# First block's states decayed on their way out of PSUM, and a work list drawn up 30 more times

## The chip, the cores and the metric

The kernel runs as one launch on 1 core of a Trainium2 chip. The metric is device time in microseconds, the median of several runs; lower is better. The engines of the core run side by side and wait for one another by semaphores: TensorE (PE in the profile, its weight loads PEld), VectorE (DVE), ScalarE (ACT), GpSimd (POOL), and SyncE (SP), which here issues every DMA.

## The reference

Three stages follow one another on 3072 tokens (4 batches of 768) with 512 features. First comes a retention attention with 8 heads of 64:

```python
state = np.zeros((B, H, D, D), dtype=np.float32)
for t in range(S):
    state = gamma[None, :, None, None] * state + np.einsum('bhd,bhe->bhde', k[:, :, t], v[:, :, t])
    y[:, :, t] = scale * np.einsum('bhd,bhde->bhe', q[:, :, t], state)
```

Then comes a layer 512 -> 2048 -> 512, whose hidden value h becomes h above 1, 0 below -1 and (h+1)^2/4 between. Then comes a layer 512 -> 1024 -> 512 with h * softmax(h), normalised to mean 0 and variance 1 and scaled by g_ln, ahead of the second product.

## The kernel before

The tokens are cut into 6 chunks of 128 per batch; chunk c of all 4 batches makes up block c. A unit u is one chunk of one batch: units 0 to 3 are block 0, 4 to 7 block 1, 8 to 15 blocks 2 and 3 (two batches of a pair are worked half a chunk at a time), and units 16 to 23 are done two at a time as "wide" steps in blocks 4 and 5. Within a unit, attention is a product of scores and values (with a table of decays, `dmat`), plus, from block 1 on, a "cross" product of the queries with the state that earlier chunks left.

The running state of each batch lies in `states`. Decay is spread over several tables: `vdec` scales keys, `xdec` is the loaded table of decays of the queries or outputs, `qdec` is `xdec` times the decay over 128 tokens (`gdec`), `gdec2` is that decay laid out for a state, and `gdec4` its square. In the kernel before:

- block 0 ends with one copy on ACT of a unit's state from PSUM (L819);
- block 1 multiplies its queries by `qdec` (L650 and L652), because the state has not been decayed yet; when block 1 adds its own sum to the state, the old state is first scaled by `gdec2` in 4 pieces on ACT (L804), and then the sum is added on DVE (L805);
- blocks 3 and 5 first multiply the state by `gdec4` on DVE (L541, in `counted_on`), so the states are held two chunks at a time; even blocks take values scaled by `vgrow` and outputs scaled by `qdec`, odd ones values scaled by `vdec` and outputs scaled by `xdec`;
- `qdec` is loaded as a copy of the table and multiplied by `gdec` on POOL (L480), early; `xdec` is loaded a second time, later (L493).

While block 0 to 3 of attention run, the first layer's products for blocks 0 and 1 (L1068 into, L1142 out) and the conversion of the weights to two parts (L393 to L428) run as well. Blocks 2 to 5 then go through a seven-product scheme (L1324, L1477), and the last layer follows (L1819, L1930, L1962).

The order on each engine is fixed when the program is built. Every piece of work is a `Task` with an engine, a cost, the tasks it depends on and a buffer that it takes. `Plan.late` walks back from the planned products of PE and gives each other task a goal, the time by which it is wanted. `Plan.listed` then plays the engines forward by the costs and always takes the ready task with the earliest goal; products of PE may be taken a few places early in the first and last parts (`loose`). `Plan.run` does this 4 times, each time with goals worked out from the list before, and keeps the list whose reckoned end of PE is earliest. The instructions are then written out in that order, and each engine works strictly in order. POOL and those DVE tasks that depend on no PE product are kept apart in the list (`port`).

Of the kernel before, what the change touches and what calls it, by code (L numbers as in the profile page):

```python
# [24 lines left out]
C = 128  # L25
# [69 lines left out]
class Plan:  # L95
# [32 lines left out]
    def run(self, rounds=4):  # L128
        best, edges, order = None, {}, list(self.tasks)
        for _ in range(rounds):  # L130
            self.late(order, edges)
            try:
                end, order, edges = self.listed()
            except RuntimeError:
                if best is None:
                    raise
                break
            if best is None or end < best[0]:
                best = end, order, [(t, t.start, t.end) for t in order]
# [126 lines left out]
def kernel(  # L266
# [189 lines left out]
    def tables():  # L456
# [21 lines left out]
        b = DMA(2, lambda: nc.sync.dma_start(gdec, gdec_d), (), -50.0)  # L478
        q = DMA(256, lambda: nc.sync.dma_start(qdec, xtab_d), (), -50.0)
        tab["qdec1"] = [POOL(1.05, lambda: gp.tensor_tensor(out=qdec, in0=qdec, in1=gdec.to_broadcast([128, NPAIR, C]), op=ALU.mult), (b, q), -48.0)]  # L480
# [5 lines left out]
    def late_tables():  # L486
# [6 lines left out]
        tab["xdec"] = [DMA(256, lambda: nc.sync.dma_start(xdec, xtab_d))]  # L493
# [9 lines left out]
    def out_factors(c):  # L503
        return (xdec, tab["xdec"]) if c % 2 else (qdec, tab["qdec1"])
# [5 lines left out]
    def scaled_values(c, p, o, swapped):  # L510
        t, deps = ((vdec2, "vdec2") if swapped else (vdec, "vdec")) if c % 2 else ((vgrow2, "vgrow2") if swapped else (vgrow, "vgrow"))
# [25 lines left out]
    def counted_on(c, pair):  # L537

        st = states[pair]
        if c % 2:  # L540
            st_wrote[pair] = [DVE(U512, lambda: ve.tensor_tensor(out=st, in0=st, in1=gdec4.to_broadcast([128, 2, NPAIR, D]), op=ALU.mult), [*st_wrote[pair], *tab["gdec4"]])]  # L541
# [87 lines left out]
    def att_scores0(u):  # L629
# [12 lines left out]
        if u >= CPB:  # L642
# [3 lines left out]
            def f():  # L646
                e["qn"] = attp.tile([128, NPAIR, C], F32, tag="qn", name="qn", bufs=NQN)
                q = e["qk"][:, 0]
                if not o:
                    ve.tensor_tensor(out=e["qn"], in0=q, in1=qdec, op=ALU.mult)  # L650
                for r in range(2) if o else ():
                    ve.tensor_tensor(out=e["qn"][64 - 64 * r:128 - 64 * r], in0=q[64 * r:64 * r + 64], in1=qdec[64 * r:64 * r + 64], op=ALU.mult)  # L652
            e["qn_task"] = DVE((1 + o) * U512, f, [e["lq"]] + tab["qdec1"], t.vend + 1, (e["qn_slot"],))
# [72 lines left out]
    def att_steps0(u):  # L726
# [76 lines left out]
        if blk:  # L803
            dec = [ACT(A64, partial(lambda p: sc.activation(st[:, p], st[:, p], AF.Copy, scale=gdec2[:, b % 2, p, :]), p), [ta] + tab["gdec"]) for p in range(NPAIR)]  # L804
            x = DVE(U256, lambda: ve.tensor_tensor(out=st, in0=e["sp"], in1=st, op=ALU.add), [tb, *dec])  # L805
# [1264 lines left out]
```

## Time and profile before

| what | us |
|---|---|
| median of 3 runs (lowest, highest) | 844.01 (843.34, 844.15) |
| the profiled execution's own time | 842.65 |
| its span, first to last instruction | 840.7 |
| PE busy | 827.5 (98%) |
| DVE busy | 679.8 (81%) |
| ACT busy | 566.6 (67%) |
| POOL busy | 133.4 (16%) |

The profiled execution took 1.95 us more than its span, and 1.36 us less than the median of the runs. A busy share says how long an engine had work under way; the end of the program is set by PE's order of products and by the gaps between them.

### The profile page before, as it was taken

Reading aid. Unit: us, or ns where it says so; the run is one execution under the profiler, and the core shown is the slowest. Engines: PE = TensorE matmul, PEld = TensorE weight load, DVE = VectorE, ACT = ScalarE, POOL = GpSimd, SP = SyncE. Lnnn points to the kernel's source line nnn. Section 1 sums busy time; section 2 is a strip of 40 time slices with the busy share of each in tenths; the row PEclk is TensorE's granted clock in tenths of the full one; section 3 lists DMA queues with packets and bytes.
Section 4 is the critical chain, followed back from the end, with each engine's and each line's share of the span. In section 5 each row is a group of like instructions: output and inputs, shape, how many; then the busy total and the mean of one; then the engine's idle time right before and its main releaser. Section 6 shows DMA issues by size and latency. Waiting matters only on the chain.

```text
span 840.7 us, 15941 instructions
## 1 busy us (share of the span) xinstructions
PE 827.5 (98%) x5872; PEld 677.1 (81%) x5872; DVE 679.8 (81%) x1299; ACT 566.6 (67%) x1107; POOL 133.4 (16%) x403
## 2 busy tenths in 40 slices
PE   9999999999999999999999999999999999999997
PEld 7778888777878888888888788887888888888885
DVE  6999999999857678999996397898777777777751
ACT  3898977897799898874588685445555555555552
POOL 1100000000000000001200000022473333333443
PEclk9999999999999999999999999999999999999999
DMA  8967999998999999876765555764202012021011
GB/s 329 399 214 242 320 313 322 335 323 301 335 374 335 347 345 327 327 282 238 228 216 196 200 197 188 265 196 159 69 33 75 27 40 61 18 71 24 15 39 37
DMA packets 66145, 175.72 MB, mean 209 GB/s; under 512 B 8338, under 2 KB 12562, under 8 KB 66068
## 3 DMA queue, kind: packets, MB, share of 16 engines
q1 hardware_dynamic: 66068, 174.71, 60.0%
q8 instruction: 46, 0.75, 0.4%
q14 instruction: 31, 0.25, 0.1%
HBM read 124.35 MB, written 50.33 MB: 208 GB/s over the span
## 4 chain that ended last, share of the span: by engine, by line
PE 67%; DVE 18%; ACT 7%; DMA 5%; issue 2%; SPq 0%; ACTq 0%; DVEq 0%
PE hp L1324 17%; PE op L1962 16%; PE yp L1477 14%; PE h2p L1819 13%; PE tp L1930 2%; PE acc L1142 2%; DMA w_raw<-in_w_in_dram 2%; DVE wm L409 2%; DVE wm L406 1%; DMA x2p<-cs 1%; DVE w L428 1%; DVE go L1444 1%; PE hp L1068 1%; DVE cs L1050 1%; DVE gl L1099 1%
## 5 line engine op out<-in xcount | busy, mean ns | idle before, releaser
L1477 PE MATMUL yp<-go,left 128*128 128x512 f32 x672 | 153.0, 389 | 0.0
L1477 PEld LDWEIGHTS yp<-go,left 128*128 128x128 f32 x672 | 126.1, 188 | 26.2
L1324 PE MATMUL hp<-xoh,left 128*128 128x512 f32 x448 | 121.8, 394 | 0.6 <-DVE g L1050 0.4
L1440 ACT ACTIVATE go<-g 128x512 fp32r<-128x512 f32 x112 | 69.8, 629 | 51.4 <-PE yp L1477 30.3
L1324 PEld LDWEIGHTS hp<-xoh,left 128*128 128x128 f32 x448 | 82.9, 188 | 19.3 <-ACT hp L1352 1.1
L1962 PE MATMUL op<-w,lh 128*128 128x512 f32 x384 | 93.5, 391 | 0.8 <-ACT lh L1937 0.8
L1819 PE MATMUL h2p<-w,x2h 128*128 128x512 f32 x336 | 92.3, 396 | 0.5 <-ACT h2p L1832 0.4
L1509 POOL TENSOR_TENSOR gl<-gl,gh 128x512 f32<-128x512 f32 x4 | 6.5, 1636 | 504.4 <-DVE gl L1506 373.4
L1962 PEld LDWEIGHTS op<-w,lh 128*128 128x128 f32 x384 | 71.9, 188 | 16.5 <-ACT lh L1937 1.5
L1444 DVE TENSOR_TENSOR go<-g,go 128x512 fp32r<-128x512 f32 x112 | 76.9, 691 | 8.2 <-ACT go L1440 7.5
L1142 PE MATMUL acc<-gh,w 128*128 128x512 f32 x256 | 69.9, 402 | 2.0 <-ACT gh L1095 1.2
L1819 PEld LDWEIGHTS h2p<-w,x2h 128*128 128x128 f32 x336 | 61.3, 188 | 13.0 <-ACT h2p L1832 1.1
L1324 PE MATMUL hp<-xol,left 128*128 128x512 f32 x224 | 69.0, 389 | 0.0
L1068 PE MATMUL hp<-xh,w 128*128 128x512 f32 x248 | 62.6, 393 | 0.6 <-DVE w L428 0.6
L1881 DVE TENSOR_REDUCE st<-h2p 128x1 f32<-128x512 f32 x24 | 16.5, 686 | 57.1 <-PE h2p L1819 57.1
L1049 ACT ACTIVATE cs<-cs 128x512 f32<-128x512 f32 x96 | 59.2, 625 | 0.9
L1142 PEld LDWEIGHTS acc<-gh,w 128*128 128x128 f32 x256 | 46.2, 188 | 13.8 <-ACT gh L1095 1.6
L1068 PEld LDWEIGHTS hp<-xh,w 128*128 128x128 f32 x248 | 45.9, 188 | 11.6 <-DVE w L428 1.4
L1047 ACT ACTIVATE cs<-hp,half 128x512 f32<-128x512 f32 x64 | 43.5, 681 | 12.9 <-PE hp L1324 7.6
L1819 PE MATMUL h2p<-w,x2l 128*128 128x512 f32 x168 | 51.8, 389 | 0.0
L1937 ACT ACTIVATE lh<-tp 128x512 fp32r<-128x512 f32 x48 | 28.4, 597 | 33.3 <-PE tp L1930 20.4
L1324 PEld LDWEIGHTS hp<-xol,left 128*128 128x128 f32 x224 | 42.0, 188 | 9.1 <-DVE xol L1268 0.2
(165 smaller groups left out, 1669.7 us busy)
## 6 DMA issues: line engine op xcount, KB each, us to landing
left<-left SPq DMA_DIRECT2D x112, 512.0 KB, 4.7
left<-wsh SPq DMA_DIRECT2D x64, 256.0 KB, 3.9
qk<-in_qk_t_dram SPq DMA_DIRECT2D x24, 512.0 KB, 6.6
w_raw<-in_w_in_dram SPq DMA_DIRECT2D x24, 512.0 KB, 6.4
w_raw<-in_w_out_dram SPq DMA_DIRECT2D x24, 512.0 KB, 7.2
left<-w SPq DMA_DIRECT2D x48, 256.0 KB, 2.8
kv<-in_kv_t_dram SPq DMA_DIRECT2D x16, 512.0 KB, 5.4
x2r<-x2d SPq DMA_DIRECT2D x12, 512.0 KB, 5.1
```

Source lines behind the costliest of these rows:

```text
L409: ve.tensor_tensor(out=c["mi"], in0=c["mi"], in1=c["p"].bitcast(I32), op=ALU.add)
L1047: sc.activation(c["t"], get_h(), AF.Relu, bias=half, scale=0.5)
L1049: q = ACT(A512, lambda: sc.activation(c["t"], c["t"], AF.Square), (r,), due + 0.5)
L1068: pe.matmul(c["h"], cut(w, part, k), r[:, k, :], start=(n == 0), stop=(n == 3 * KD - 1))
L1142: pe.matmul(banks[d], cut(w, l, d), r, start=(first and fresh and n == 0), stop=(last and n == 2), skip_group_check=True)
L1324: pe.matmul(e[bank], w[i][:, k * 128:(k + 1) * 128], x[j][:, k], start=(first and m == 0), stop=(last and m == 3 * KH - 1), skip_group_che ...
L1440: sc.activation(t[:, 0], quarters_g(n)[q], AF.Copy)
L1444: ve.tensor_tensor(out=lo, in0=quarters_g(n)[q], in1=fl(hi), op=ALU.subtract)
L1477: pe.matmul(e["banks"][j], w[:, s, j * 128:(j + 1) * 128], g[t], start=(n == 0 and c == 0), stop=(n == NP - 1 and c == 2))
L1819: pe.matmul(bank[b], x[t][:, AT[key], k], w2i[key, k]["w"][:, part], start=(start and m == 0), stop=(stop and m == 3 * KH - 1), skip_group ...
L1937: sc.activation(c["h"][:, 4 * n:4 * n + 4], c["tp"][:, n].rearrange("a (j c) -> a j c", j=4), AF.Copy)
L1962: pe.matmul(o["p"], c[l][:, f_], w2o[f_]["w"][:, part], start=(k == 0 and f_ == 0), stop=(k == 2 and f_ == NF2 - 1))
```

## The change

Block 0's states are scaled by `gdec2` when they are copied from PSUM, in 4 pieces on ACT instead of one whole copy. Block 1 then multiplies its queries by `xdec` as it was loaded, and adds its sum to the state without scaling it. The states are therefore carried on at blocks 2 (by `gdec2`) and 4 (by `gdec4`) instead of 3 and 5, and even and odd blocks swap their tables. `xdec` is loaded once, early; `qdec` is made from it later, in 4 pieces on ACT, and the multiplication on POOL is gone.

`Plan.run` goes on for 30 more rounds: in each, the goals of the best list so far are moved by up to 0.2 us either way, by a fixed rule of the task's number and the round, for every task that is not PE's, and the list is made again. The list with the earliest reckoned end is kept.

```diff
-    def run(self, rounds=4):
+    def run(self, rounds=4, more=30, shift=0.2):
         best, edges, order = None, {}, list(self.tasks)
-        for _ in range(rounds):
-            self.late(order, edges)
+        for r in range(rounds + more):
+            if r < rounds:
+                self.late(order, edges)
+            else:
+                for n, (t, goal) in enumerate(zip(self.tasks, best[3])):
+                    if t.eng != "PE":
+                        t.goal = goal + shift * ((n * 7919 + r * 104729) % 1009 / 504.5 - 1.0)
+            goals = [t.goal for t in self.tasks]
             try:
                 end, order, edges = self.listed()
             except RuntimeError:
                 if best is None:
                     raise
-                break
+                continue
             if best is None or end < best[0]:
-                best = end, order, [(t, t.start, t.end) for t in order]
+                best = end, order, [(t, t.start, t.end) for t in order], goals
...
-        b = DMA(2, lambda: nc.sync.dma_start(gdec, gdec_d), (), -50.0)
-        q = DMA(256, lambda: nc.sync.dma_start(qdec, xtab_d), (), -50.0)
-        tab["qdec1"] = [POOL(1.05, lambda: gp.tensor_tensor(out=qdec, in0=qdec, in1=gdec.to_broadcast([128, NPAIR, C]), op=ALU.mult), (b, q), -48.0)]
+        tab["gdec1"] = [DMA(2, lambda: nc.sync.dma_start(gdec, gdec_d), (), -50.0)]
+        tab["xdec"] = [DMA(256, lambda: nc.sync.dma_start(xdec, xtab_d), (), -50.0)]
...
-        tab["xdec"] = [DMA(256, lambda: nc.sync.dma_start(xdec, xtab_d))]
+        tab["qdec"] = [ACT(A128, partial(lambda p: sc.activation(qdec[:, p], xdec[:, p], AF.Copy, scale=gdec[:, p]), p), [*tab["gdec1"], *tab["xdec"]]) for p in range(NPAIR)]
...
     def out_factors(c):
-        return (xdec, tab["xdec"]) if c % 2 else (qdec, tab["qdec1"])
+        return (qdec, tab["qdec"]) if c % 2 else (xdec, tab["xdec"])
...
-        t, deps = ((vdec2, "vdec2") if swapped else (vdec, "vdec")) if c % 2 else ((vgrow2, "vgrow2") if swapped else (vgrow, "vgrow"))
+        t, deps = ((vgrow2, "vgrow2") if swapped else (vgrow, "vgrow")) if c % 2 else ((vdec2, "vdec2") if swapped else (vdec, "vdec"))
...
-        st = states[pair]
-        if c % 2:
-            st_wrote[pair] = [DVE(U512, lambda: ve.tensor_tensor(out=st, in0=st, in1=gdec4.to_broadcast([128, 2, NPAIR, D]), op=ALU.mult), [*st_wrote[pair], *tab["gdec4"]])]
+        st, g = states[pair], gdec4 if c > NOLD else gdec2
+        if c % 2 == 0:
+            st_wrote[pair] = [DVE(U512, lambda: ve.tensor_tensor(out=st, in0=st, in1=g.to_broadcast([128, 2, NPAIR, D]), op=ALU.mult), [*st_wrote[pair], *tab["gdec4"]])]
...
-                    ve.tensor_tensor(out=e["qn"], in0=q, in1=qdec, op=ALU.mult)
+                    ve.tensor_tensor(out=e["qn"], in0=q, in1=xdec, op=ALU.mult)
...
-            e["qn_task"] = DVE((1 + o) * U512, f, [e["lq"]] + tab["qdec1"], t.vend + 1, (e["qn_slot"],))
+            e["qn_task"] = DVE((1 + o) * U512, f, [e["lq"]] + tab["xdec"], t.vend + 1, (e["qn_slot"],))
...
-            dec = [ACT(A64, partial(lambda p: sc.activation(st[:, p], st[:, p], AF.Copy, scale=gdec2[:, b % 2, p, :]), p), [ta] + tab["gdec"]) for p in range(NPAIR)]
-            x = DVE(U256, lambda: ve.tensor_tensor(out=st, in0=e["sp"], in1=st, op=ALU.add), [tb, *dec])
+            x = DVE(U256, lambda: ve.tensor_tensor(out=st, in0=e["sp"], in1=st, op=ALU.add), [ta, tb])
...
-            x = ACT(A256, lambda: sc.activation(st, e["sp"], AF.Copy), (tb,))
-            st_wrote[b // 2].append(x)
-            sp_slot.used(x)
+            x = [ACT(A64, partial(lambda p: sc.activation(st[:, p], e["sp"][:, p], AF.Copy, scale=gdec2[:, b % 2, p, :]), p), (tb, *tab["gdec"])) for p in range(NPAIR)]
+            st_wrote[b // 2] += x
+            sp_slot.used(*x)
```

## Rows read from the trace of the kernel before

**Rows 1.** The page's first line: the span.

```profile
span 840.7 us, 15941 instructions
```

**Rows 2.** Busy time by stretch (us, count), granted clock, DMA share, GB/s.

```profile
0.00:65.00 65.00, 61.41 (x615) 49.61 (x616) 56.52 (x106) 46.83 (x111) 7.42 (x11) 0.97 0.84 312
65.00:240.00 175.00, 172.30 (x1686) 138.51 (x1685) 166.78 (x323) 142.12 (x286) 0.00 (x0) 1.00 0.92 316
240.00:800.00 560.00, 558.83 (x3411) 461.03 (x3410) 441.58 (x839) 362.93 (x687) 111.34 (x337) 1.00 0.51 176
800.00:841.00 41.00, 34.94 (x166) 27.97 (x164) 14.89 (x32) 14.72 (x27) 14.64 (x56) 0.97 0.15 33
```

**Rows 3.** Waits of PE, 0 to 65 us: total, times, longest.

```profile
PE pa L742 <- DVE qn L650: 0.8, 1, 0.8
PE hp L1068 <- DVE w L428: 0.6, 1, 0.6
PE pa L742 <- DVE sm L664: 0.4, 1, 0.4
```

**Rows 4.** Waits of PE, 62 to 240 us.

```profile
PE acc L1142 <- ACT gh L1095: 1.2, 1, 1.2
PE pa L690 <- DVE xr L879: 0.7, 1, 0.7
PE acc L1142 <- ACT acc L1125: 0.7, 2, 0.4
```

**Rows 5.** Timeline, 20.8 to 26.8 us: start, length, engine, line; idle before and releaser.

```profile
20.87 1.20 SPq L482 DMA_DIRECT2D gdec<-in_gdec_dram  x2
20.92 2.49 POOL L606 TENSOR_TENSOR kv<-kv,vdec 128x512 f32<-128x512 f32 x2 [2.03 <-DMA kv<-in_kv_t_dram]
...
23.08 0.37 ACT L819 ACTIVATE state<-sp 128x256 f32<-128x256 f32 x1
...
23.38 1.22 POOL L480 TENSOR_TENSOR qdec<-qdec,gdec 128x512 f32<-128x512 f32 x1
...
23.73 1.15 DVE L403 TENSOR_SCALAR wm<-wm 128x512 uint32<-128x512 uint32 x1
...
24.80 0.68 DVE L428 TENSOR_TENSOR w<-wm,w 128x512 fp32r<-128x512 f32 x1
...
25.53 1.20 PE L1068 MATMUL hp<-xh,w 128*128 128x512 f32 x4 [0.55 <-DVE w L428]
...
26.71 0.63 ACT L1095 ACTIVATE gh<-cs 128x512 fp32r<-128x512 f32 x1 [1.89 <-DVE cs L1050]
```

**Rows 6.** Timelines of DVE and of ACT behind that.

```profile
28.73 0.68 DVE L650 TENSOR_TENSOR qn<-qk,qdec 128x512 f32<-128x512 f32 x1
...
31.16 1.06 ACT L804 ACTIVATE state<-state,gdec 128x64 f32<-128x64 f32 x4
```

**Rows 7.** Groups by line, shapes apart: count, busy us, mean ns, idle before.

```profile
L403 DVE TENSOR_SCALAR wm<-wm 128x512 uint32<-128x512 uint32 x48 | 21.0, 442 | 0.2
...
L1781 ACT ACTIVATE x2h<-x2r 128x256 fp32r<-128x256 f32 x36 | 14.5, 405 | 0.0
...
L804 ACT ACTIVATE state<-state,gdec 128x64 f32<-128x64 f32 x16 | 4.5, 337 | 0.0
...
L541 DVE TENSOR_TENSOR state<-state,gdec 128x512 f32<-128x512 f32 x4 | 2.8, 688 | 0.0
...
L819 ACT ACTIVATE state<-sp 128x256 f32<-128x256 f32 x4 | 1.4, 372 | 0.0
```

**Rows 8.** Busy time in stretches of 20 us, columns as in Rows 2.

```profile
40.00:60.00 20.00, 19.57 (x179) 15.33 (x178) 19.92 (x39) 19.80 (x50) 0.00 (x0) 1.00 0.64 223
60.00:80.00 20.00, 20.00 (x125) 16.42 (x124) 20.00 (x41) 16.76 (x34) 0.00 (x0) 1.00 0.70 230
...
100.00:120.00 20.00, 20.00 (x265) 16.11 (x264) 19.95 (x38) 15.23 (x32) 0.00 (x0) 1.00 0.87 296
```

**Rows 9.** The tiles named gdec: from a DMA's issue to its landing.

```profile
DMA to landing us min/median/max: 5.1/6.1/6.9
```

More of the change, by code (lines that the diff above doesn't have):

```diff
@@ L649, in f @@
                 if not o:
-                    ve.tensor_tensor(out=e["qn"], in0=q, in1=qdec, op=ALU.mult)
+                    ve.tensor_tensor(out=e["qn"], in0=q, in1=xdec, op=ALU.mult)
                 for r in range(2) if o else ():
-                    ve.tensor_tensor(out=e["qn"][64 - 64 * r:128 - 64 * r], in0=q[64 * r:64 * r + 64], in1=qdec[64 * r:64 * r + 64], op=ALU.mult)
-            e["qn_task"] = DVE((1 + o) * U512, f, [e["lq"]] + tab["qdec1"], t.vend + 1, (e["qn_slot"],))
+                    ve.tensor_tensor(out=e["qn"][64 - 64 * r:128 - 64 * r], in0=q[64 * r:64 * r + 64], in1=xdec[64 * r:64 * r + 64], op=ALU.mult)
+            e["qn_task"] = DVE((1 + o) * U512, f, [e["lq"]] + tab["xdec"], t.vend + 1, (e["qn_slot"],))
             e["qk_slot"].used(e["qn_task"])
```

## The prediction, made before the changed kernel ran

> **What bounds the kernel now.** I read the span and the busy times first, then PE's busy time by stretch, then the list of who PE waited for, then the timelines around the longest early waits. PE is busy for nearly all of the span [rows 1, 2]. The four stretches of [rows 2] show where it is not: 65 - 61.41 = 3.59 us idle up to 65 us, 2.70 us from 65 to 240, 1.17 us in the 560 us after that, and about 6 us in the last stretch, where the program runs out. The reader is to see that the last layers, over 500 us long, have next to nothing to give. All that a better order could return, short of fewer products, is the idle time of the first three stretches, 7.46 us or 0.9% of the span, part of which is the start before the first product. 0.2% of the median is 1.69 us, about what a measurement of this kernel can tell from no change; so a gain that can be told needs about a quarter of that idle time.
>
> The early idle time has names [rows 3]: the first cross product of block 1 waits 0.8 us for its scaled queries (L650), a product of the first layer 0.6 us for a converted weight (L428), another cross product 0.4 us for masked scores. From 62 to 240 us the waits go to ACT (1.2 us for `gh`, 0.7 us in two for reloaded sums) and to DVE's `xr` (0.7 us) [rows 4]. None of these names a state (L805, L819, L804, L541). The waits in which this change could matter are the first two of [rows 3].
>
> **The multiplication that leaves POOL.** DVE's L403 takes 442 ns on average [rows 7], but the one at 23.73 us takes 1.15 us [rows 5]. It starts while POOL multiplies `qdec` (23.38 to 24.60 us) and ends just behind it. The excess is 1.15 - 0.44 = 0.71 us. L428 comes next on DVE, at 24.80, and PE's product waits for it for 0.55 us [rows 5]. Without the POOL instruction the two earlier POOL instructions (20.92 to 23.41) are over when L403 starts, so L428 comes up to 0.71 us earlier and the whole 0.55 us goes. I take -0.55; the bounds are -0.55 and 0, the latter if the list puts other work there.
>
> **The queries.** L650 starts at 28.73 [rows 6], in DVE's order, after a factor that POOL had ready at 24.60. In the changed kernel it needs the loaded table and the queries alone, so it may go ahead of something. But if PE and DVE both come earlier by the same 0.55 us, the 0.8 us [rows 3] stays. Bounds 0 and -0.8. Nothing in the rows shows which of the two; I take the middle, -0.4.
>
> **ACT.** Per unit of blocks 0 and 1, four pieces that take 1.06 us in a row [rows 6] and one whole copy of 0.37 us [rows 7] become four pieces. The trace has no piece of 128x64 read from PSUM. From below it costs what four from SBUF do, 1.06 us; from above four whole copies, 4 x 0.372 = 1.49 us. I take 1.06, the row with the same size. That removes 0.37 us per unit, 1.5 us over the four pairs of units. The four pieces of `qdec`, 128x128, lie between 337 ns (128x64) and 405 ns (128x256) each [rows 7], 1.3 to 1.6 us in all, and stand later. In sum ACT's work stays the same to within 0.4 us.
>
> Its place changes. The first two copies, at 23.08 and a little later [rows 5], each grow by 1.06 - 0.37 = 0.69 us, 1.4 us together, ahead of the first `gh`. The cover is ACT's own idle time of 1.89 us before that `gh` [rows 5]: cost nothing; with that cover gone, up to 1.4 us on `gh` and then on the products of L1142. In exchange block 1's groups of 1.06 us, the first at 31.16 us [rows 6], leave ACT in a time that takes in its fullest stretch, 19.80 of 20 us [rows 8]. No wait of PE before 65 us is put down to them [rows 3], so I take 0 for this as well. The four pieces of `qdec` come after 65 us, where ACT has 4.8 of 20 us free from 100 to 120 us [rows 8]: 0, and at most their own 1.6 us if they stood right ahead of something that PE wanted.
>
> **DVE.** The four multiplications of a pair's states (688 ns each [rows 7]) stay four, but move from blocks 3 and 5 to blocks 2 and 4. Two of them now fall where DVE is busy 19.95 of 20 us [rows 8]. PE waits there for nothing that DVE makes [rows 4], so DVE's fullness there is work done ahead, and the multiplication only pushes that back: 0; if a block's scores stood behind one, +0.69 us a pair, +1.4 in all. What leaves block 3 could give the same back, in a stretch where PE does wait for DVE (0.7 us for `xr` [rows 4]): bounds -0.7 and +1.4, taken as 0. The swaps of `vdec` with `vgrow` and of `xdec` with `qdec` keep count and shape: 0.
>
> **DMA.** The table is loaded once instead of twice, 256 KB fewer. No wait of PE in [rows 3, 4] is put down to a load: 0, bounds 0 and the 0.4 us of the smallest early wait, as a gain.
>
> One load matters more than before. `gdec2` must now have landed before the first copy of a state. Its last two parts are issued from 20.87 us on [rows 5], and such loads of 1 to 2 KB take up to 6.9 us to land [rows 9]: 27.8 us, against a first copy at 23.08. Left so, ACT would stand still for 4.7 us. By the Trainium skill (DMA: Bandwidth & Descriptors, "Anatomy of one DMA") a DMA costs about 2.0 us plus its bytes' time, so that by an estimate from that page the load would be there at 22.9 us and cost nothing. The trace says three times as much, with other loads queued ahead, and the trace decides. The list works the load's goal back from its first user, and the early places on SP of the load of `qdec` and of `gdec`, which nothing early needs any more, come free; so I expect `gdec2` to be issued 4 or 5 us earlier, and cost nothing. If it is not, that is the third rival below.
>
> **The list.** Thirty more lists can only be kept if the reckoned end is earlier. What that is worth on the chip no row shows. From below it is the idle time that [rows 2] leave in the second and third stretch, 2.70 + 1.17 = 3.87 us, all gone; from above a new wait as long as the longest that the old list left, +1.2 us [rows 4]. Since waits left over may come from durations that the list has wrong, which no shift of goals cures, I take little: a sixth of 3.87, -0.6 us.
>
> **Sum.** -0.55 - 0.4 - 0.6 = -1.55 us. The profiled execution becomes 842.65 - 1.55 = 841.1; the median of the runs stands 1.36 us above it, so 842.46, for which I say 842.4.
>
> **Rivals.**
> First, the freed time carries no further (chance 0.17): DVE is full from 60 to 80 us and again from 100 to 120 [rows 8], and what PE gains at 25 us it loses at the next wait for DVE or for the reloaded sums. For it: the waits of [rows 4] are for engines that do not start earlier because PE does. Against it: PE's waits behind 62 us are few, so that little stands ready to take the gain back. Time 844.0, 843.4 to 844.6.
>
> Second, the list finds much more than I took (0.15): half or more of the 3.87 us and both early waits. -0.55 - 0.8 - 2.0 = -3.35 and beyond: 840.7, down to 839.5. For it: the second stretch has only a handful of waits, each of which one exchange of two instructions could end. Against it: four rounds have been over the same ground.
>
> Third, slower (0.13): the states wait for `gdec2`. ACT works strictly in order, so behind a copy that waits stand the activations that lead to `gh`, and behind them DVE's `gl` and PE's L1142. 4.7 us of waiting less the 1.89 us of idle time ahead of `gh` [rows 5] leaves +2.8 us, and with the -0.55 us it is about +2.3: 846.3. It decides from the point where `gdec2` lands over 1.89 us behind the first copy's turn, or over 0.5 us if the longer copies have eaten 1.4 us of that. Against it: only a badly reckoned load would bring it about.
>
> **Chances.** The main case, a sum between -0.6 and -3.0 us, has 0.55; its likeliest value is just under what can be told, so I put 0.28 of it within 0.2% and 0.27 beyond. With the second rival, faster by over 0.2% has 0.27 + 0.15 = 0.42; with the first, within 0.2% has 0.28 + 0.17 = 0.45; slower has 0.13. The main case's own range is 841.0 to 843.4. The range for 8 in 10 takes in the first rival and most of the second: 840.0 to 845.0; it leaves out the third and a little of the second.
>
> **What would show it.** L403 or its like near 24 us back at 0.44 us, and no instruction of POOL at L480's place; L428's wait gone from PE's list; L650's wait at most 0.8 us; the pieces of the first states at 1.06 us a group, with no idle time of ACT ahead of them put down to a DMA; PE's idle time from 65 to 240 us no longer than 2.70 us. The prediction is wrong if an early wait for `gdec2` or for `gh` shows up, if the second stretch has new waits of over a microsecond, or if the last layers change by over 1 us, which nothing here explains.

## The result, and the profile after

The changed kernel took 851.88 us (median of 6 runs, 850.22 to 856.20) beside 844.08 us (6 runs, 842.38 to 845.88) for the kernel before. The ratio is 1.0107, with a 95% interval of 1.009 to 1.0123: slower, by 7.6 to 10.4 us of 844, where 842.4 was forecast. One kernel below (sums_old_order) was disturbed in two of its ten executions, the profiled one among them (span 1031 us); these two are left out and its trace is not read, and the same kernel was run again as old_list_again.

The profiled execution after took 850.71 us. First its windows by stretch, with the columns of [rows 2]:

```profile
0.00:65.00 65.00, 60.43 (x588) 49.37 (x590) 54.13 (x103) 45.63 (x112) 6.26 (x10) 0.95 0.75 284
65.00:240.00 175.00, 171.57 (x1705) 138.07 (x1700) 167.75 (x324) 140.70 (x278) 0.00 (x0) 1.00 0.93 316
240.00:800.00 560.00, 555.53 (x3385) 455.99 (x3386) 437.36 (x822) 361.23 (x684) 113.30 (x328) 1.00 0.52 179
800.00:849.00 49.00, 43.24 (x203) 34.88 (x201) 21.72 (x53) 19.88 (x35) 16.98 (x64) 1.00 0.15 33
```

PE stands idle 4.57, 3.43 and 4.47 us in the first three stretches, where [rows 2] had 3.59, 2.70 and 1.17. No stretch holds the whole loss, and the largest growth, 3.3 us, is in the third, which was to have next to nothing to do with it. Idle time explains 5.0 us in these three; PE's busy time grew as well, from 827.5 to 830.8 us, and one reason for that stands below. Then who PE waited for, over the whole span (total, times, longest):

```profile
PE pa L646 <- issue: 2.1, 1, 2.1
PE pa L986 <- issue: 1.9, 1, 1.9
PE hp L1330 <- ACT hp L1358: 1.7, 1, 1.7
PE acc L1148 <- ACT acc L1131: 1.4, 1, 1.4
PE pa L697 <- DVE xr L885: 1.1, 1, 1.1
```

Line numbers are 6 to 8 higher than before. None of these five waits stands in [rows 3, 4] at such a length, and only two have a counterpart there: `acc` (0.7 in two) and `xr` (0.7).

Where the time went is best read from landmarks. The view of one line gives the first and the last start of its products (durations in ns, then first and last start in us). Before:

```profile
L1324 PE MATMUL hp<-xoh,left x448: 387/389/504, 239.5 to 492.9; 128*128 128x512 f32 x150
L1477 PE MATMUL yp<-go,left x672: 389/389/398, 334.2 to 565.4; 128*128 128x512 f32 x168
L1819 PE MATMUL h2p<-w,x2h x336: 389/389/504, 565.7 to 810.1; 128*128 128x512 f32 x168
L1962 PE MATMUL op<-w,lh x384: 387/389/502, 585.7 to 833.7; 128*128 128x512 f32 x192
```

After:

```profile
L1330 PE MATMUL hp<-xoh,left x448: 389/389/504, 242.4 to 499.7; 128*128 128x512 f32 x150
L1483 PE MATMUL yp<-go,left x672: 387/389/492, 339.3 to 572.2; 128*128 128x512 f32 x168
L1825 PE MATMUL h2p<-w,x2h x336: 389/389/500, 572.5 to 818.4; 128*128 128x512 f32 x168
L1968 PE MATMUL op<-w,lh x384: 387/389/500, 592.2 to 842.1; 128*128 128x512 f32 x192
```

The first `xoh` product comes 2.9 us late, the first `yp` product 5.1, the first `h2p` product 6.8, the last `op` product 8.4. So 2.9 us were lost up to 242 us, 2.2 up to 339, 1.7 up to 572 and 1.6 in the last layers. These four landmarks serve for every kernel below.

What the prediction said of the first 30 us did come about. Timeline after, DVE and then PE:

```profile
23.55 0.43 DVE L411 TENSOR_SCALAR wm<-wm 128x512 uint32<-128x512 uint32 x1
23.89 0.68 DVE L436 TENSOR_TENSOR w<-wm,w 128x512 fp32r<-128x512 f32 x1
```

```profile
23.62 2.19 PE L1074 MATMUL hp<-xh,w 128*128 128x512 f32 x8
28.38 2.11 PE L1074 MATMUL hp<-xh,w 128*128 128x512 f32 x8 [0.56 <-ACT w L428]
31.32 1.09 PE L749 MATMUL pa<-qn,state 64*64 64x128 f32 x16
```

The decoding step that took 1.15 us in [rows 5] is back at 0.43, the product no longer stops for 0.55 us, and the cross product that waited 0.8 us for its queries waits no more. But a later product of the same kind already stops for 0.56 us, for a part of a weight that ACT makes, and ten microseconds later all of the gain is lost. PE around 34 us, then ACT and DVE:

```profile
33.27 0.63 PE L768 MATMUL pa<-kv 128*64 128x64 f32 x16
35.95 1.64 PE L646 MATMUL pa<-qk 64*128 64x128 f32 x16 [2.06 <-issue]
```

```profile
32.59 1.14 ACT L825 ACTIVATE state<-sp,gdec 128x64 f32<-128x64 f32 x5
33.95 0.60 ACT L798 ACTIVATE xh<-pa 128x512 fp32r<-128x512 f32 x1 [0.21 <-PE pa L768]
...
34.84 0.42 DVE L811 TENSOR_TENSOR state<-pa,state 128x256 f32<-128x256 f32 x1
35.17 0.68 DVE L804 TENSOR_TENSOR xl<-pa,xh 128x512 fp32r<-128x512 f32 x1
```

The new list sends the next unit's scores (L646) straight behind the states (L768); the old one had twelve products of L1142 between them. The scores start 0.10 us behind the end of L804, which reads a PSUM tile of the same pool; the profile names no releaser ("issue"), so that this tile is the one waited for is inferred from the times.

This stop costs more than its length. Behind it the granted clock of TensorE falls to half (1.2 instead of 2.4 GHz) from 36.5 to 39.9 us. The window of after from 36 to 40 us (clock third from the end), then eight products of after in it, and the same eight of after_block, a kernel below with the same list, where the clock stayed at full speed:

```profile
36.00:40.00 4.00, 4.00 (x22) 3.29 (x23) 2.82 (x6) 4.00 (x12) 0.00 (x0) 0.57 1.03 404
```

```profile
37.53 3.17 PE L1148 MATMUL acc<-gh,w 128*128 128x512 f32 x8
```

```profile
37.97 2.11 PE L1148 MATMUL acc<-gh,w 128*128 128x512 f32 x8
```

With the scores ahead of them (1.64 us instead of 1.16) that is 1.5 us, which no list of waits shows. Of the 2.9 us by which the first `xoh` product is late, 1.7 us are more idle time and most of the rest is this. In the 15 traces read here there are nine such falls between 15 and 800 us, and each begins within 1.7 us of the end of one of PE's longest stops (1.8 to 3.4 us): one in after, after_420, after_shift, after_swap (423 us), list_alone (280 us), sums_alone (285 us) and mended (239 us), two in new_then_old (38 and 123 us). Seven other stops of that length, four of them in after_block, had none behind them.

### The profile page after: what moved, and what is told of

Its sections match the earlier page's. It is cut to its first block, busy times and chain, and to the rows that moved or that the text cites. A ratio compares the mean times of both kernels' runs of the same rounds, so it can differ in the third digit from the quotient of the medians.

```text
span 848.9 us, 15924 instructions
## 1 busy us (share of the span) xinstructions
PE 830.8 (98%) x5872; PEld 678.3 (80%) x5872; DVE 681.0 (80%) x1299; ACT 567.4 (67%) x1107; POOL 136.5 (16%) x402
## 4 chain that ended last, share of the span: by engine, by line
PE 76%; DVE 11%; DMA 5%; ACT 3%; issue 2%; POOL 1%; SPq 1%; ACTq 0%; POOLq 0%; DVEq 0%
PE hp L1330 18%; PE yp L1483 17%; PE op L1968 13%; PE h2p L1825 11%; PE hp L1074 5%; PE acc L1148 5%; PE tp L1936 2%; DMA qk<-in_qk_t_dram 2%; DMA w_raw<-in_w_in_dram 1%; DVE ws L1216 1%; DVE xol L1274 1%; DVE w L436 1%; DVE wsh L1230 1%; DMA kv<-in_kv_t_dram 1%; DVE gl L1105 1%
## 5 line engine op out<-in xcount | busy, mean ns | idle before, releaser
L1330 PE MATMUL hp<-xoh,left 128*128 128x512 f32 x448 | 121.8, 393 | 2.3 <-ACT hp L1358 1.7
L1330 PEld LDWEIGHTS hp<-xoh,left 128*128 128x128 f32 x448 | 82.9, 188 | 21.0 <-ACT hp L1358 2.2
L1515 POOL TENSOR_TENSOR gl<-gl,gh 128x512 f32<-128x512 f32 x4 | 9.0, 2258 | 509.8 <-DVE gl L1512 376.7
L1148 PE MATMUL acc<-gh,w 128*128 128x512 f32 x256 | 71.0, 406 | 1.4 <-ACT acc L1131 1.4
L1330 PE MATMUL hp<-xol,left 128*128 128x512 f32 x224 | 69.0, 389 | 0.0
L1148 PEld LDWEIGHTS acc<-gh,w 128*128 128x128 f32 x256 | 47.1, 191 | 13.2 <-ACT acc L1131 2.2
L1330 PEld LDWEIGHTS hp<-xol,left 128*128 128x128 f32 x224 | 42.0, 188 | 9.0
```

The lines of the kernel that those rows point to most:

```text
L1148: pe.matmul(banks[d], cut(w, l, d), r, start=(first and fresh and n == 0), stop=(last and n == 2), skip_group_check=True)
L1330: pe.matmul(e[bank], w[i][:, k * 128:(k + 1) * 128], x[j][:, k], start=(first and m == 0), stop=(last and m == 3 * KH - 1), skip_group_che ...
```

## The experiments

**Theory.** The sums as changed cost nothing; what costs is that the program gets another list, whose small waits no reckoning of the list's end saw. **Rival.** The changed sums cost by themselves: longer state copies, another wait, more work for a full engine.

All medians are shown beside the kernel before on the same chip; the ratio compares the means of the runs, so it is not quite the quotient of the medians. The landmarks and DVE's busy time between 20 and 150 us (of 130) are each kernel's own rows of the views shown above. They belong to one execution each, which can lie some 3 us from the median: old_then_new's was the fastest of nine (844.03), list_alone's and sums_alone's were the slowest of theirs. In shaken, mended_twice and after_swap the four products ahead of the first scores took 3.78 us, in the others 1.98 to 2.31, and PE is about 2 us late at 20 us for that alone: so much of the lateness in these three rows is not the list's.

| kernel | list, sums | median us (runs); before | ratio, 95% interval | DVE busy 20-150 | 1st `xoh` | 1st `yp` | 1st `h2p` | last `op` |
|---|---|---|---|---|---|---|---|---|
| before | old, old | | | 127.80 | 239.5 | 334.2 | 565.7 | 833.7 |
| list_alone | 30 more, old | 846.14 (7); 843.67 | 1.0030, 1.0016-1.0043 | 126.18 | 240.4 | 339.2 | 570.4 | 839.2 |
| shaken | one more, old | 846.50 (8); 843.67 | 1.0031, 1.0017-1.0046 | 126.96 | 241.2 | 335.9 | 567.6 | 837.8 |
| sums_alone | 4 rounds, new | 848.70 (5); 843.67 | 1.0052, 1.0031-1.0073 | 123.72 | 245.0 | 343.6 | 574.8 | 842.8 |
| sums_old_order | old, new | 844.03 (8); 843.67 | 0.9994, 0.9980-1.0008 | | | | | |
| old_list_again | old, new | 842.09 (12); 843.57 | 0.9978, 0.9961-0.9995 | 127.07 | 238.6 | 334.4 | 565.7 | 833.8 |
| after | 30 more, new | 851.88 (6); 844.08 | 1.0107, 1.0090-1.0123 | 124.96 | 242.4 | 339.3 | 572.5 | 842.1 |
| old_then_new | old to 236 us, new | 846.81 (9); 843.02 | 1.0046, 1.0033-1.0060 | 127.44 | 237.7 | 332.7 | 565.8 | 835.4 |
| new_then_old | new to 236 us, old | 849.03 (5); 843.02 | 1.0054, 1.0030-1.0078 | 121.88 | 245.6 | 340.9 | 572.1 | 840.2 |
| after_swap | after, one place | 852.84 (4); 843.02 | 1.0109, 1.0092-1.0126 | 126.23 | 243.5 | 340.5 | 575.4 | 845.1 |
| after_420 | after, one place | 851.11 (4); 843.71 | 1.0099, 1.0072-1.0125 | 124.71 | 242.7 | 337.4 | 569.9 | 839.6 |
| after_shift | after, shifted | 851.73 (4); 843.02 | 1.0092, 1.0067-1.0117 | 123.75 | 244.1 | 340.0 | 572.6 | 842.3 |
| after_block | after, shifted | 849.98 (4); 843.71 | 1.0069, 1.0053-1.0085 | 123.96 | 244.6 | 339.3 | 572.7 | 842.4 |
| dve_load | old, DVE work added | 845.40 (10); 843.71 | 1.0025, 1.0012-1.0037 | 126.12 | 243.1 | 337.8 | 569.0 | 837.0 |
| mended | old, mended; new | 848.22 (9); 843.71 | 1.0042, 1.0021-1.0063 | 127.73 | 243.3 | 338.8 | 570.0 | 838.1 |
| mended_twice | old, mended; new | 844.31 (12); 843.57 | 1.0005, 0.9988-1.0022 | 126.76 | 241.9 | 338.1 | 569.3 | 837.4 |

### List or sums

The list alone: the old sums, with the thirty more lists (`run` as in the diff of the change, nothing else of it).

```diff
-    def run(self, rounds=4):
+    def run(self, rounds=4, more=30, shift=0.2):
```

> The sums of the kernel before, with the 30 more lists. The list's own reckoned end of PE falls from 821.36 to 820.23 us. If the new sums cost the time (they raise the reckoned end to 823.18 with four rounds), this kernel is at or under the kernel before: 842 to 844.5. If it is the further lists that cost, it is at 848 to 853. If any list that is made anew costs some microseconds, because the list of before stood well on the chip by luck, it is at 845 to 850 although its reckoned end is the earliest of all.

The sums alone: the kernel after with `run` as it was.

```diff
-    def run(self, rounds=4, more=30, shift=0.2):
+    def run(self, rounds=4):
```

> The new sums with the four rounds of the kernel before; reckoned end 823.18, 1.82 us later than before, where the changed kernel has 822.52. If the new sums cost the time, 849 to 853. If the further lists cost it, 842.5 to 845. If any new list costs, 846 to 852.

A list made once more, for the old sums, with goals moved by up to 0.2 us, and kept whatever its end:

```diff
-        for _ in range(rounds):
-            self.late(order, edges)
+        for r in range(rounds + 1):
+            if r < rounds:
+                self.late(order, edges)
+            else: (the goals of the best list, moved)
...
-            if best is None or end < best[0]:
+            if best is None or end < best[0] or r == rounds:
```

> The sums of the kernel before, and its list made once more with goals moved by up to 0.2 us and kept whatever its end: reckoned 821.83, 0.47 us later than before. If the reckoned end tells the time on the chip, 844 to 845. If any new list costs, 846 to 851: then waits stand in the trace that the list does not reckon with, at other places than before.

The new sums by the old list, written out; the four pieces of a state stand where its copy stood:

```diff
-    def run(self, rounds=4, more=30, shift=0.2):
+    ORDER = "..."
+    def run(self):
+        for n in np.frombuffer(zlib.decompress(base64.b64decode(Plan.ORDER)), np.uint16):
+            self.tasks[n].fn()
```

> The new sums, but no list is made: every piece of work stands where the list of the kernel before had it, the pieces of a state in the place of its one copy, the loads of gdec2 in the early place of the load of gdec, the four multiplications of states some 3 to 4 us ahead of the scores that need them, the four pieces of qdec at the place of 103 us. If the new sums themselves cost the time (pieces on ACT, PSUM held longer), 848 or more. If only the order costs, 842 to 844.5: the POOL multiplication is gone, so the wait of 0.55 us behind it should go, as the prediction had it.

> The changed sums by the list of the kernel before, unmended, for a trace of its own and beside the mended list on one chip. Theory (the changed sums cost nothing): within 0.3% of before, 843 to 844, no stand at 34, 120, 278 or 420 us and none in the last layers, TensorE level with before or up to 1.8 us ahead from 240 us on. Rival (the changed sums cost by themselves): 2 us or more above before.

The new sums by the old list are at 0.9994 and, on another chip, 0.9978: no loss, perhaps a small gain. The old sums by a new list lose 0.3% twice, once with a list that is by construction reckoned to end no later than the old one, once with one that is only shaken. That decides for the list and against the rival. It also says why leaving the thirty lists out does not help: changed tasks force a new list, and the four rounds' own costs 0.5%. Nor does the reckoned end order the lists: the ends named in the expectations are 820.23 us for list_alone, 821.36 for before, 821.83 for shaken, 822.52 for after and 823.18 for sums_alone, and the losses 2.5, 0, 2.8, 7.8 and 5.0 us of the median. A new list cost the new sums two to three times what it cost the old ones; why is open.

How the early gain goes when the old list is kept shows in old_list_again. DVE, PE and ACT there (a written-out list puts its lines 69 to 73 higher than before):

```profile
23.71 0.43 DVE L474 TENSOR_SCALAR wm<-wm 128x512 uint32<-128x512 uint32 x1
...
25.93 0.69 DVE L1119 SCALAR_TENSOR_TENSOR cs<-cs,hp 128x512 f32<-128x512 f32 x1 [0.59 <-ACT cs L1118]
...
28.67 0.68 DVE L720 TENSOR_TENSOR qn<-qk,xdec 128x512 f32<-128x512 f32 x1
...
24.18 2.11 PE L1137 MATMUL hp<-xh,w 128*128 128x512 f32 x8
...
29.50 1.09 PE L812 MATMUL pa<-qn,state 64*64 64x128 f32 x16 [1.22 <-DVE qn L720]
...
23.06 0.91 ACT L888 ACTIVATE state<-sp,gdec 128x64 f32<-128x64 f32 x4
...
24.42 0.96 ACT L888 ACTIVATE state<-sp,gdec 128x64 f32<-128x64 f32 x4
25.21 0.69 ACT L1118 ACTIVATE cs<-cs 128x512 f32<-128x512 f32 x1
```

The product's stop is gone, but DVE's L1119 waits 0.59 us behind ACT's two groups of pieces, and the queries start at 28.67 us, 0.06 earlier than in [rows 6]. PE waits for them 1.22 us instead of 0.8: the gain is over at 30 us.

### Early or late

The two lists were joined at 236 us of planned time, with the new sums in both.

> The changed sums; the first 236 us by the list of the kernel before, the rest by the list of the kernel after. Theory (the new list loses time place by place, and each stretch has its own loss): the kernel after was 2.9 us behind at 240 us and 8.3 at the end, so this one loses the other 5.4 us: 849.5, with the stand in the 64x64 products near 278 us, the one at about 420 us and the short ones of the last layers. Rival (the late losses only pass on what came late out of the first stretch): about 844. If the second half of the sums is at fault rather than the list: also 849.5, which the next kernel tells apart.

> The changed sums; the first 236 us by the list of the kernel after, the rest by the list of the kernel before. Theory: 844 + 2.9 = 847, with the 2.1 us stand of the scores near 34 us and none at 278, 420 and in the last layers. Rival (what comes late out of the first stretch makes the later stands): about 852. If the list had nothing to do with it in either stretch, both mixtures would be alike.

The early part of the new list costs 0.54%, the late part 0.46%; together 1.00%, beside the 1.07% of the whole. The landmarks say the same. Old_then_new, in the fastest of its executions, reaches the first `xoh` product at 237.7 us, 1.8 ahead of before, and ends 1.7 behind: 3.5 us lost behind it, with the wait of 1.7 us at L1358's place once more. New_then_old is 6.1 us late at that landmark, with two falls of the clock ahead of it, and 6.5 at the end. Each part loses on its own, and what comes late out of the first is neither caught up nor made worse in the second.

### What bounds the early part

PE is behind by about as much as DVE stood idle. Between 20 and 150 us DVE is busy 127.80 us before, in the five kernels that run the new list's early part unaltered (after, after_420, after_shift, after_block, new_then_old) 121.88 to 124.96. The first `xoh` product is at 239.5 us there and at 242.4 to 245.6 here, latest in the one where DVE was idle longest, new_then_old. That alone does not say which engine holds the other up: a late PE leaves DVE idle too. One place, after, DVE and then PE:

```profile
119.54 0.42 DVE L885 TENSOR_TENSOR xr<-pa,xdec 128x256 f32<-128x256 f32 x1
...
120.78 0.69 PE L697 MATMUL pa<-qk 64*64 64x64 f32 x32 [1.09 <-DVE xr L885]
```

DVE works without a pause from 100 us to here, so `xr` is late because DVE is. Where it had stood shows in its own waits (after, 20 to 150 us):

```profile
DVE state L811 <- ACT xh L798: 2.0, 2, 1.5
DVE cs L1056 <- ACT cs L1055: 1.3, 2, 0.8
DVE sm L671 <- PE pa L646: 1.2, 1, 1.2
```

The last of them is PE's stand at 34 us, handed on. Whether DVE really bounds the stretch was tried with the old list and the new sums, five decoding steps (L428 of before) done twice between 55 and 75 us:

```diff
             self.tasks[n].fn()
+            if n in (211, 98, 149, 220, 355):
+                self.tasks[n].fn()
```

> The changed sums by the list of the kernel before, with five VectorE instructions of the weights' decoding (L428 of before, 0.69 us each, one every 0.60 us) between about 55 and 75 us done twice, with the same result. Theory (VectorE bounds the stretch from 40 to 150 us): TensorE comes 5 x 0.60 = 3.0 us late out of it and the time is 843.5 + 3.0 = 846.5. Rival (TensorE bounds it and VectorE's work is hidden): 843.5, no change.

PE then waits for DVE where it had not (dve_load, 50 to 85 us):

```profile
PE hp L1139 <- DVE cs L1121: 1.7, 1, 1.7
```

The first `xoh` product comes at 243.1 us, 4.5 behind old_list_again (0.8 of it lost before 45 us, ahead of the first added step), the last `op` product 3.2 behind, and the ratio is 1.0025 beside 0.9994 and 0.9978 without the added steps: 0.31% or 0.47%, 2.6 to 4.0 us, where five steps at one every 0.60 us make 3.0. So DVE bounds PE where the steps were added, from 55 to 75 us, and its time there is carried to the end; that it does so up to 150 us is inferred from the busy times.

### Single places of the new list

After_swap puts the twelve products back ahead of the scores at 34 us, and DVE's masking of these scores behind two other steps:

```diff
   states (L768)
-  scores of the next unit (L646)
   products (L1148) x12
+  scores of the next unit (L646)
   DVE:
-  L671, L408, L1056
+  L408, L1056, L671
```

> The kernel after with one place of its list changed: the 12 products of L1148 at 37.5 us go ahead of the scores of L646, as the list of the kernel before had them. Theory (the scores stood 2.06 us for a PSUM bank that VectorE still read, and this carries to the end): that wait goes and the time is 2 us shorter, 849.9. Rival (the work behind takes it up): the wait goes and the time stays at 851.9.

The wait of 2.06 us is gone; a product of L1148 stops 0.44 us for a state's copy instead. The time is no better, 852.84. Its profiled execution is one of the three that started about 2 us late (the four products of L474 took 3.78 us instead of 2.11), and yet its first `xoh` product is only 1.1 us behind that of after: in this one execution about 1 us of the place was kept up to there. At 421 us PE stops for 2.1 us, where after had stopped for 1.73, and this time the clock falls behind the stop. The four runs don't show the 2 us that were expected.

After_420 exchanges two entries of DVE. In the kernel after, DVE, ACT and PE there:

```profile
417.95 2.32 DVE L1274 TENSOR_TENSOR xol<-xr,xoh 128x1024 fp32r<-128x1024 f32 x1
420.20 0.68 DVE L1532 TENSOR_TENSOR cs<-yp,cs 128x512 f32<-128x512 f32 x1
...
420.97 0.58 ACT L1358 ACTIVATE hp<-hp 128x512 f32<-128x512 f32 x1 [1.84 <-DVE cs L1532]
...
421.60 1.20 PE L1330 MATMUL hp<-xoh,left 128*128 128x512 f32 x4 [1.73 <-ACT hp L1358]
```

```diff
-  L1274 (xol), L1532 (cs)
+  L1532 (cs), L1274 (xol)
```

> The kernel after with one pair of its list exchanged: at 418 us VectorE adds the token sums of L1532 before it makes the low part of L1274 (2.32 us there). Theory (each place of the new list costs by itself): TensorE's wait of 1.73 us for L1358 at 420 us goes and stays gone, 851.9 - 1.7 = 850.2. Rival (another wait takes its place): 851.9.

PE's line there, in after_420:

```profile
419.45 0.73 PE L1393 MATMUL hp<-xol,left 128*128 128x512 f32 x2 [0.56 <-DVE xol L1337]
```

The wait for L1358 is gone, and the pushed-back `xol` makes one of 0.56. From the first `yp` to the first `h2p` product are 231.5 us before, 233.2 after and 232.5 here: 0.7 of the 1.7 us came back. The median, 851.11, lies among runs from 848.27 to 854.45 and decides nothing.

The third large wait, 1.90 us inside the 64x64 products, waits for no semaphore. After:

```profile
276.53 1.15 PE L979 MATMUL pa<-sm,kv 64*64 64x64 f32 x62
...
280.50 0.34 PE L986 MATMUL pa<-kv 64*64 64x64 f32 x7 [1.90 <-issue]
```

PE's instructions come by a DMA queue of their own, 46 loads and 0.75 MB by the page, 16 KB each. In after one of them falls in the window from 276 to 280 us, that of the stand (queue, kind: packets, MB, share):

```profile
q8 instruction: 1, 0.02, 1.5%
```

It starts at 278.13 us, 0.56 behind the first product of L986. In after_420, which has no such stand, the load starts at 274.29, 3.6 us ahead of that product.

Two kernels shift every later instruction of PE, with the list untouched:

```diff
-        for n in range(WARM):
-            pe.matmul(wps[:, :128], wz, wz, ...)
+        for n in range(WARM + 64):
+            k = 128 if n < 16 else 32
+            pe.matmul(wps[:, :k], wz, wz[:, :k], ...)
```

> The kernel after with its list untouched, and 104 short warm-up products at the very start in place of 40 (16 of 128 columns and 88 of 32, about as many columns in all), so that every later TensorE instruction stands 64 products further on in its instruction stream. Theory of the instruction stream (the 1.90 us stand inside the 64x64 products near 278 us, which waits for no semaphore, is TensorE's next block of instructions arriving late, and depends on where the blocks end): that stand is gone or shorter, about 850 us, unless another block ends badly. Rival (the stand comes from the order of the list or from the data transfers beside it): it stays as long and the time is 851.9.

For after_block, 128 more, all of 32 columns.

> The kernel after with its list untouched and 168 warm-up products of 32 columns in place of 40 of 128, so that every later TensorE instruction stands 128 products further on, twice the shift of the last one. Theory of the instruction stream (the stand in the 64x64 products near 278 us depends on where the blocks of TensorE's instructions end, and a block is as long as 128 products with their weight loads): the blocks end where they ended in the kernel after, and the stand of 1.9 us is back, which the shift of 64 products had taken away; 851.9. Rival (where the blocks end has nothing to do with it, and the stand comes and goes by chance): it may be missing here as it was there.

After_shift has no stand in the 64x64 products, but one of 0.9 us without a semaphore in L1330, near 260 us. After_block, where the theory wanted it back, has none at all, and neither has after_420, which shifts nothing. So the stand comes and goes from one execution to the next. What it goes with shows in the starts of that load in all 15 traces, against the first product of L986 or its like. Where the load starts 0.4 to 1.0 us behind it (after, after_swap, list_alone, sums_alone), PE stands 1.7 to 2.1 us; where it starts 0.1 to 0.8 ahead (old_list_again and the two kernels below), 0.5 to 1.0; where it starts 1.6 to 3.7 ahead (the other eight), not at all there. Each stand, that in L1330 too, ends 2.2 to 2.6 us behind the start of a load. The old list has it too, though shorter: 0.8 us in old_list_again, 0.5 and 1.0 in the two kernels below. It is no mark of the new list, but it makes up the 2.2 us that after lost between `xoh` and `yp`: from the one landmark to the other are 94.7 us before, 96.9 after, and 94.7 again in after_420 and after_block.

### Mending the old list

If waits of the list carry to the end, taking some out should beat both kernels. Twice the new sums were run by the old list with a few entries of ACT and DVE moved (lines of before):

```diff
   86 us   DVE: ... L409,
-    L1050 (waits for L1049), L403, L400, L406, L1099, L400, L403, L409, L1050, L403, L409, L1099, L1194
+    L403, L406, L1050, L400, L403, L400, L1099, L409, L1194, L1050, L403, L409, L1099
   229 us  ACT: L1047,
-    L1264, L1049, L532 x2, L1047, L1095, L1049, L1264, L1095
+    L1049, L1047, L1095, L1049, L1264, L1095, L532 x2, L1264
   229 us  DVE:
-    L1268, L1050, L1245, L1099, L1050
+    L1050, L1099, L1050, L1268, L1245
```

> The changed sums by the list of the kernel before, with two places of that list put in another order and no work changed: at 86 us VectorE's decoding steps that are ready go ahead of the L1050 that waited 1.19 us for ScalarE; at 229 to 235 us ScalarE makes gh before the 1024-wide xoh and the second block's queries, so that the products of L1142 do not wait 1.18 us. Theory (VectorE bounds the stretch from 40 to 150 us, so that its idle time there carries to the end, and a PE wait at 233 us carries too): 843.0 - 1.0 - 1.2 = 840.8, and nearer 840 if the changed sums still bring the 1.7 us that the trace of the old-then-new list showed by 240 us. Rival (something behind takes it up): 843, as with the list of before alone.

The second keeps the place at 86 us, leaves the mistake of the first at 229 us out and adds the place at 192 us:

```diff
   192 us  DVE: L428,
-    L409, L1099, L400, L879, L891, L879
+    L1099, L879, L879, L409, L400, L891
   192 us  ACT:
-    L420, L1047
+    L1047, L420
   229 us  ACT: L1047,
-    L1264, L1049, L532 x2, L1047, L1095, L1049, L1264, L1095
+    L1049, L1095, L1264, L1047, L1049, L532, L1095, L532, L1264
   229 us  DVE:
-    L1268, L1050, L1245, L1099, L1050, L1268, L1099
+    L1050, L1099, L1268, L1050, L1099, L1245, L1268
```

> The changed sums by the list of the kernel before, with three places put in another order and no work changed: the one at 86 us as in the mended list; at 192 us VectorE's two xr steps go ahead of a decoding step, for the 0.69 us that TensorE waits at 195 us; at 229 to 235 us both gh and both gl are made before the work that nobody waits for yet (the mended list had left the second gl behind a 1024-wide step, and TensorE waited 3.43 us for it). Theory (a wait that is really taken away, with none put in its place, carries to the end): TensorE is 0.7 + 1.2 us earlier than with the unmended list from 240 us on, and 0 to 1 us more by the place at 86 us, so 2 to 3 us under the unmended list of this call, 841 to 842. Rival (the next late work behind each place takes its gain up): no different from the unmended list, 843.5.

The first took 848.22 us. Its trace says why, DVE and PE:

```profile
237.43 1.22 DVE L1337 TENSOR_TENSOR xol<-xr,xoh 128x1024 fp32r<-128x1024 f32 x1 [1.12 <-ACT xoh L1333]
238.57 0.68 DVE L1168 TENSOR_TENSOR gl<-cs,gh 128x512 fp32r<-128x512 f32 x1
...
239.31 0.72 PE L1211 MATMUL acc<-gl,w 128*128 128x512 f32 x1 [3.43 <-DVE gl L1168]
```

`gh` came early as meant, and its `gl` stood behind a wide step that waited for the `xoh` just moved back. Behind this stop, too, the clock fell to half, from 239.4 to 242.8 us. The second took 844.31 us, against 842.09 for the unmended list on the same chip. The two waits of PE that it was made for (0.6 us for `xr` and 1.0 for `gh` in old_list_again) are gone, and between 150 and 300 us three others stand there:

```profile
PE pa L919 <- DVE xr L948: 1.7, 1, 1.7
PE hp L1393 <- ACT cs L1225: 1.2, 1, 1.2
PE pa L1049 <- issue: 1.0, 1, 1.0
```

Of the 3.3 us by which its first `xoh` product is behind that of old_list_again, about 2 are the late start of this execution. The theory of that expectation fails, and its rival, no difference, is the nearer: what was won at a place was taken up by the next, and the median came out 2.2 us above the unmended list's. The old list with the new sums, unmended, is the best that was run, at 0.9994 and 0.9978.

## Why the prediction was wrong

**The list, -0.6 us: the step that failed.** It was priced by the idle time that the old list had left, and bounded from above by "a new wait as long as the longest that the old list left, +1.2 us". Both take the new list for the old one with small repairs. It is another list: PE's own order differs at 10 of 598 places, DVE's at 690 of 1294. Nor was it one with an earlier reckoned end: the thirty lists started from the four that the new sums had given, and the best of them was reckoned to end at 822.52 us, 1.16 later than the old list's 821.36. The prediction took the thirty lists for a gain without comparing the two. Its five longest waits are 2.1, 1.9, 1.7, 1.4 and 1.1 us, 8.2 us in all, four of them (6.3 us) the list's own; and the price of a new list for the old sums is +2.5 us (list_alone) and +2.8 us (shaken). For the new sums it was the whole +7.8 us, since by the old list they lose nothing. The reckoned end is no guide: list_alone's is 1.13 us earlier than before's, and it lost 2.5 us. That a long stop can cost a fall of the clock on top of its length, 1.5 us at 36 us, was in neither bound. Nor was it seen that the changed tasks force a new list by themselves.

**"DVE's fullness there is work done ahead."** This was the reason for pricing DVE's moved work at nothing and for the first rival's small range. It is wrong where it was tried, from 55 to 75 us: dve_load lost 2.6 to 4.0 us for 3.0 us of added work. For 100 to 120 us, of which the prediction said it, no run tried it. If DVE bounds PE there too, a DVE that stands idle for 2 us costs 2 us, though PE waits for nothing at that moment; the idle time of the new list's early part goes with its lateness in five traces, but was not taken away by itself.

**The sums, -0.95 us.** By the old list they bring 0.06% and 0.22%, 0.5 and 1.9 us, the first not clear of nothing; the size fits as far as that can be told. The way does not: the 0.55 us of the POOL multiplication do come, and are gone at the next cross product, and the queries' 0.4 us do not come by that list at all. What there is comes later, by 160 to 240 us (the first `xoh` product 0.9 and 1.8 us earlier). Which of the moved terms brings it was not taken apart.

**ACT at nothing.** The price of the pieces was right (0.91 and 0.96 us for four, 1.06 expected). The cover was not all there: by the old list they push L1118 back and DVE waits 0.59 us.

**The states waiting for `gdec2`: right that they don't.** In the list after, the parts of `gdec` are issued between 16.4 and 18.7 us, 2 to 4.5 us earlier than in [rows 5], and no copy of a state is held up by a DMA. The 2.0 us that the prediction set beside its rows from the Trainium skill (DMA: Bandwidth & Descriptors, "Anatomy of one DMA") stand there for DMAs that GpSimd issues. Here SP issues them, and the loads of `gdec` took 2.4 to 7.1 us to land after, 5.7 in the median.

**What would show it wrong** was named rightly: new waits of over a microsecond in the second stretch (1.4 and 1.1), and the last layers: 268.0 us from the first `h2p` to the last `op` product before, 269.6 after, and 269.6 to 269.7 in each kernel with the new list's late part (old_then_new, after_420, after_block), 268.1 with the old one's. That step is the list's too; it is spread over short waits and was not traced to one entry.

The second rival's lower end, 839.5 us, does not come out of its terms, which give 844.0 - 0.55 - 0.8 - 3.87 = 838.8; nothing hangs on it.

## What to carry to other kernels

A change that makes a planner write a new order is two changes: price the order apart, by running the new work in the old order and the old work in a new one. Where an order already stands within 1% of full, expect another to cost rather than to gain: each newly made list here cost 0.3 to 1.1%, and why the old one stood so well is not known. Choose among orders by their time on the chip, not by a reckoned end or by removing one wait at a time. Look for the engine that works without a pause ahead of the waits: its idle time can be what PE pays for, later and elsewhere. And look at the granted clock behind each long stop of PE.

## What was not expected of the hardware

In 8 of the 15 traces read here PE stops once between 240 and 300 us, for 0.5 to 2.1 us, with no semaphore awaited, seven times in the run of 64x64 products; each stop ends 2.2 to 2.6 us behind the start of a load of PE's instructions. The Trainium skill (Runtime: NRT & Kernel Launch, "Instruction fetch mechanics") says that instructions come in 16 KiB blocks, fetched while the current one executes, at a cost mostly hidden. The 46 loads of 16 KB agree with the first part; the stop of 1.90 us is one that is not hidden. That the late load is its cause rests on the order of the 15 traces, the later the load the longer the stop, and not on a run that moved a load by itself. Why the load comes late in one execution and in time in the next stays open.

The granted clock fell from 2.4 to 1.2 GHz nine times in the midst of these programs, each time shortly behind a long stop of PE, and stayed at 2.4 GHz behind seven stops as long; which of the two it will be stays open as well.
